# Moving two inverse groups, the W2 split and W4's first loads in a one-core S4 convolution and channel-mixing kernel

## The chip, the cores and the metric

The kernel runs on one core of a Trainium2 chip. Its engines work at the same time, each through its own instructions in order: PE (TensorE, matmuls; PEld are its weight loads), DVE (VectorE), ACT (ScalarE), POOL (GpSimd) and SP (SyncE, which here only issues DMAs). They wait for each other by semaphores. The metric is device time in microseconds (us) of one execution, lower is better; the number that counts is the median of several timed runs.

## The reference

Input `u` is 2048 x 512 (sequence x channels), all in float32. Cut to what matters:

```python
mod = (_silu(c) @ w_mod).reshape(c.shape[0], 6, 1, -1)
sa, ca, ga, sb, cb, gb = (mod[:, 0], mod[:, 1], mod[:, 2], mod[:, 3], mod[:, 4], mod[:, 5])
h = _layernorm(x, axis=-1) * (1 + ca) + sa
x = x + ga * S4(h)            # long convolution along the sequence, by rfft / irfft of length 4096
h = _layernorm(x, axis=-1) * (1 + cb) + sb
x = x + gb * MLP(h)

def MLP(x):
    h = _gelu(_layernorm(x) @ w1)                  # 512 x 512
    hs = shift_quarters(h, (+1, -1, +2, -2)) @ w2  # each quarter of the channels shifted along the sequence
    x1 = x + hs
    return x1 + _gelu(_layernorm(x1) @ w3) @ w4    # 512 x 1376, 1376 x 512
```

## The kernel before

The whole kernel is one function, `body`, whose instructions are written in the order in which each engine takes them (`tc.manual_schedule()`), so the place of a call in the code is its place in every queue. A value read by matmul at full precision is held as two parts, a rounded high one and the rest (`w1h`/`w1l`, `nh`/`nl`, `wh`/`win`); a product then takes three matmuls per tile. Its stages:

1. **Kernel and input spectra, first half** (to about 207 us): the convolution kernel is built by sines and exponentials, `u` is normalized and transformed, partial spectra go to a scratch tensor `VU`. Loads without a reader nearby hang in `side[k]`, calls made behind turn `k` of a loop of 33. Among them POOL copies `w3` and `w4` in eight pieces into scratch tensors (`WD`, traced as `Dw`, L519).
2. **16 spectrum steps** (loop at L1096; `n` 0 to 15, two halves `jh` of the channels, eight `kc` each). In step `n`, PE makes the kernel's spectrum (`spectrum_k`, L667), DVE the complex product (`multiply`: `ma`, `mb` at L678 and L679, `zc` at L683), PE transforms the product of the step before back (`back`, L693, evicted to `z` by ACT and stored to `ZT`), then makes the input's spectrum of the next step (`spectrum_u`, L644, evicted to `us`). `load_inv` brings one group of `ZT` for the last transform, and `inverse(jh, g)` does it: 8 matmuls in the code, each traced as two (L722, tiles `py` and `ld`), then two adds on DVE into `X2`, the running sum `x` (traced as `KX`, L725). There are four groups `g` in each half. Groups 0, 1, 2 of half 0 stand in steps 11, 12, 13, group 3 behind the loop. W1 and W2 are loaded in halves into a `ld` block by SP (L738), and split one step later: ACT rounds to `w1h`/`w2h` (L120, the line of all ACT operations), DVE takes the difference (L744). W1 is split in steps 9 and 10, the first half of W2 in step 15, its second half in the head.
3. **The head** (L1141 to L1250): the second half's groups arrive from `ZT`, and meanwhile the token mixer starts on groups of 256 tokens in the order 7, 0, 1, 2, 3. `keep(n)` (L1139) issues `n` matmuls whose result nobody reads. `half_stat` and `first_stats` take the statistics of `x` (L772, L777 and L758, L759; POOL finishes them to `rs`, L753 and L754). `mix_mod1` and `mix_mod2` modulate on DVE (L762, L765) and take new statistics, POOL makes `rs` and `nm` of them, `mix_norm` normalizes on ACT (`h`), `transposed` turns `h` on PE (L790, into `pT0` and `pT1`), `parts_of` splits it into `nh` (ACT) and `nl` (DVE, L798), `mix_half` multiplies by W1 (L825, L826 and L828; tile `pm`) and stores the result `go` to the scratch tensor `GD`, in SP's queue (L837). For groups 7 and 0 POOL also copies a halo (L846 to L852). `chan_load` reads the shifted quarters back (`win`, L860), `chan_split` splits them, `chan_sum` multiplies by W2 (L879 to L882). `load_w(c)` loads a third of W3 and of W4 from the scratch tensors in place, into the tile that becomes the low part; `split_w` splits later.
4. **Eight channel groups** (`chan`, from about 391 us): the remaining tokens through W1, W2, W3 and W4.

`ldp` is a ring of 7 blocks of 512 KB for `vu`, W1, W2 and the loads of `ZT`; a load waits until the readers of the block seven places back are through. `psy` holds two tiles `py`. An inverse half takes one of them until its add is done.

## Time and profile before

| | |
|---|---|
| median of 3 timed runs | 710.89 us (709.84 to 711.97) |
| the profiled execution | 707.85 us |
| its span, first to last instruction | 706.1 us |
| PE busy | 668.3 us, 95% of the span |
| DVE, ACT, POOL busy | 500.5, 335.6, 91.8 us |
| granted TensorE clock | 1.00 throughout |
| DMA | 85.51 MB, mean 121 GB/s |

Rows of a timeline give the start in us, the time in us, engine, line of the code, operation, output tile `<-` inputs, shapes and count; a bracket gives how long the engine idled ahead of it and what ended that. Rows of the chain give start, time and what it was. A busy engine is only of interest where others wait for it: each step and each stretch of the head has its own.

### The profile page before, as it was taken

Reading aid. Unit: us, or ns where it says so; the run is one execution under the profiler, and the core shown is the slowest. Engines: PE = TensorE matmul, PEld = TensorE weight load, DVE = VectorE, ACT = ScalarE, POOL = GpSimd, SP = SyncE. Lnnn points to the kernel's source line nnn. Section 1 sums busy time; section 2 is a strip of 40 time slices with the busy share of each in tenths; the row PEclk is TensorE's granted clock in tenths of the full one; section 3 lists DMA queues with packets and bytes.
Section 4 is the critical chain, followed back from the end, with each engine's and each line's share of the span. In section 5 each row is a group of like instructions: output and inputs, shape, how many; then the busy total and the mean of one; then the engine's idle time right before and its main releaser. Section 6 shows DMA issues by size and latency. Waiting matters only on the chain.

```text
span 706.1 us, 16836 instructions
## 1 busy us (share of the span) xinstructions
PE 668.3 (95%) x7083; PEld 516.8 (73%) x7083; DVE 500.5 (71%) x827; ACT 335.6 (48%) x553; POOL 91.8 (13%) x203
## 2 busy tenths in 40 slices
PE   1999999999999999997999899999999999999997
PEld 0456655665578665663778789899898988989896
DVE  7899999999986766867888868467454536354522
ACT  3978898888956354541443632314132221213120
POOL 4011121021000010001562101001110000000000
PEclk9999999999999999999999999999999999999999
DMA  8903274636349996955468111011110201011011
GB/s 281 291 3 94 78 213 120 181 102 194 70 122 337 269 284 234 337 193 198 163 204 293 61 31 31 16 51 26 46 44 16 64 13 38 23 31 31 0 31 31
DMA packets 56627, 85.51 MB, mean 121 GB/s; under 512 B 5508, under 2 KB 43400, under 8 KB 54888
## 3 DMA queue, kind: packets, MB, share of 16 engines
q1 hardware_dynamic: 52536, 66.87, 33.1%
q0 software_dynamic: 3136, 16.52, 6.6%
q8 instruction: 56, 0.92, 0.6%
q10 hardware_dynamic: 880, 1.05, 0.5%
q14 instruction: 19, 0.16, 0.1%
HBM read 58.20 MB, written 31.85 MB: 128 GB/s over the span
## 4 chain that ended last, share of the span: by engine, by line
PE 48%; DMA 2%; DVE 2%; ACT 1%; issue 1%; SPq 0%; POOL 0%; ACTq 0%; DVEq 0%
PE pm L825 7%; PE pm L826 7%; PE pm L828 7%; PE pa L949 6%; PE pa L941 6%; PE pa L942 6%; PE ph L879 2%; PE ph L880 2%; PE ph L882 2%; PE pT L790 2%; DMA ld<-ZT 1%; PE pT L1139 1%; PE py L722 1%; DMA GD<-go 0%; DMA win<-GD 0%
## 5 line engine op out<-in xcount | busy, mean ns | idle before, releaser
L120 ACT ACTIVATE gh<-pm 128x512 fp32r<-128x512 f32 (+1 forms) x48 | 26.9, 561 | 200.6 <-PE pm L828 200.6
L825 PE MATMUL pm<-nh,w3h 128*128 128x256 f32 (+1 forms) x352 | 85.8, 279 | 0.9 <-ACT nh L120 0.9
L826 PE MATMUL pm<-nh,w3l 128*128 128x256 f32 (+1 forms) x352 | 85.6, 279 | 0.1
L933 DVE TENSOR_TENSOR gl<-gf,gh 128x512 fp32r<-128x512 f32 (+1 forms) x48 | 30.9, 643 | 68.3 <-ACT gf L120 68.3
L941 PE MATMUL pa<-w4h,gh 128*128 128x512 f32 (+1 forms) x176 | 69.6, 395 | 0.0
L942 PE MATMUL pa<-w4l,gh 128*128 128x512 f32 (+1 forms) x176 | 68.9, 392 | 0.0
L825 PEld LDWEIGHTS pm<-nh,w3h 128*128 128x128 f32 (+1 forms) x352 | 65.3, 185 | 2.6 <-ACT nh L120 1.1
L826 PEld LDWEIGHTS pm<-nh,w3l 128*128 128x128 f32 (+1 forms) x352 | 65.2, 185 | 2.2 <-DVE w3l L744 0.5
L828 PE MATMUL pm<-nl,w3h 128*128 128x256 f32 (+1 forms) x352 | 54.8, 277 | 0.0
L949 PE MATMUL pa<-w4h,gl 128*128 128x512 f32 (+1 forms) x176 | 48.1, 390 | 0.8 <-DVE gl L933 0.8
L753 POOL TENSOR_TENSOR rs<-mv,eps_t 128x1 f32<-128x1 f32 (+1 forms) x39 | 11.9, 305 | 278.3 <-DVE mv L759 266.5
L457 PE MATMUL xx<-MG,ON 64*128 64x512 f32 x160 | 47.0, 389 | 0.0
L458 PE MATMUL xx<-MG,ON 64*128 64x512 f32 x160 | 47.0, 389 | 0.0
L828 PEld LDWEIGHTS pm<-nl,w3h 128*128 128x128 f32 (+1 forms) x352 | 46.6, 185 | 0.2 <-DVE nl L798 0.2
L885 DVE TENSOR_TENSOR h<-h,ph 128x512 f32<-128x512 f32 x16 | 11.0, 687 | 45.1 <-PE ph L882 45.1
L120 ACT ACTIVATE z<-pz 128x512 f32<-128x512 f32 x32 | 17.4, 594 | 50.5 <-issue 23.2
L475 DVE SCALAR_TENSOR_TENSOR e<-tr,p 128x512 f32<-128x512 f32 x64 | 41.1, 683 | 0.4 <-ACT tr L120 0.4
L678 DVE TENSOR_TENSOR ma<-pk,us 128x512 f32<-128x512 f32 x32 | 21.9, 686 | 25.8 <-issue 13.2
L507 PEld LDWEIGHTS kp<-e,e 128*32 128x32 f32 x2048 | 30.1, 110 | 13.1 <-issue 6.8
L949 PEld LDWEIGHTS pa<-w4h,gl 128*128 128x128 f32 (+1 forms) x176 | 33.0, 188 | 8.3 <-DVE gl L933 1.2
L485 DVE TENSOR_TENSOR e<-tr,m 128x1024 f32<-128x1024 f32 x32 | 39.0, 1219 | 0.0
L484 DVE TENSOR_TENSOR e<-tr,p 128x1024 f32<-128x1024 f32 x32 | 39.0, 1219 | 0.0
(230 smaller groups left out, 1754.6 us busy)
## 6 DMA issues: line engine op xcount, KB each, us to landing
VU<-vs SPq DMA_DIRECT2D x64, 128.0 KB, 3.3
ld<-VU SPq DMA_DIRECT2D x16, 512.0 KB, 12.0
ZT<-z POOLq DMA_DIRECT2D x15, 512.0 KB, 6.0
ld<-ZT SPq DMA_DIRECT2D x12, 512.0 KB, 5.5
Dw<-in_w POOLq DMA_DIRECT2D x8, 688.0 KB, 4.7
xu<-in_u SPq DMA_DIRECT2D x16, 256.0 KB, 8.1
KX<-in_u SPq DMA_DIRECT2D x16, 256.0 KB, 12.1
GD<-go SPq DMA_DIRECT2D x16, 256.0 KB, 2.2
```

The source lines that it names most:

```text
L120: return S.activation(out, in_, f, bias=bias, scale=scale)
L457: T.matmul(x[:, :512], la, ma, start=(i == 0), stop=(i == len(ops) - 1))
L458: T.matmul(x[:, 512:], lb, mb, start=(i == 0), stop=(i == len(ops) - 1))
L475: V.scalar_tensor_tensor(e0[:, 1, a], tr[:, 1, 0], 1.0 - 2.0 * a, mg[:, a], op0=OP.mult, op1=OP.mult)
L484: V.tensor_mul(e0[:, 0], tr[:, 0, 0:1].to_broadcast([128, 2, 512]), mg)
L485: V.tensor_mul(e1.rearrange("p r d q -> p r (d q)"), tr[:, :, 1], m1s[0][:, u % 2:u % 2 + 1].to_broadcast([128, 2, 512]))
L825: T.matmul(p, wh[:, k, c], hi[k], start=(k == 0), stop=False)
L826: T.matmul(p, wl[:, k, c], hi[k], start=False, stop=False)
L828: T.matmul(p, wh[:, k, c], lo[k], start=False, stop=(k == 3))
L941: T.matmul(acc[i], gh[:m, e, s], W4h[:m, f], start=(f == 0), stop=False)
L942: T.matmul(acc[i], gh[:m, e, s], W4l[:m, f], start=False, stop=False)
L949: T.matmul(acc[i], gl[:m, e, s], W4h[:m, f], start=False, stop=(f == 10))
```

## The change

- Inverse group 1 of half 0 leaves step 12: its matmuls are issued in step 15 between the last two `back`s, its adds behind the loop's last DVE work. Group 2 leaves step 13 and stands behind the last `back`, ahead of group 3. Their loads are issued in steps 13 and 14.
- W2 is copied by POOL into a scratch tensor in the first stage (two more calls in `side`), loaded from there in step 12, straight into the tile that becomes its low part, and split in steps 14 and 15.
- `half_stat` of blocks 0 to 3 moves from the head into step 12. `keep(14)` becomes `keep(6)`, `keep(22)` becomes `keep(14)`.
- In the head, one `transposed` order changes (both tiles of one half of `h` first), two inverse halves of group 2 of half 1 change places with parts of the mixer, `mix_mod2(2, 0)` and `mix_mod2(3, 0)` go ahead of the transposes and `nl` of the group before.
- `load_w` is divided: the first third of W4 is loaded behind `chan_load(0)` instead of ahead of two `GD` stores.

```diff
-    WD = {k: dpool.tile(list(A[k].shape), F32, name="D" + k) for k in ("w3", "w4")}
+    WD = {k: dpool.tile(list(A[k].shape), F32, name="D" + k) for k in ("w2", "w3", "w4")}
...
+    for k in range(2):
+        side[28 + 3 * k].append(lambda i=k * 256: P.dma_start(WD["w2"][i:i + 256], A["w2"][i:i + 256]))
...
+    def inverse_parts(jh, g):
+        return [inv_half(jh, g, i, psy, "py") for i in range(2)]
+
     def inverse(jh, g):
-        for i in range(2):
-            inv_half(jh, g, i, psy, "py")()
+        for f in inverse_parts(jh, g):
+            f()
...
-        for k in range(4):
+        for j in range(2):
             for i in range(2):
-                T.transpose(ps[k // 2][:, k % 2, i * 128:i * 128 + 128], x[:, i, k * 128:k * 128 + 128], ident)
+                for k in range(2 * j, 2 * j + 2):
+                    T.transpose(ps[j][:, k % 2, i * 128:i * 128 + 128], x[:, i, k * 128:k * 128 + 128], ident)
...
-                W2h, W2l, ldw2 = weights(pw2, A["w2"], 512, 512, "w2", 4)
+                W2h, W2l, ldw2 = weights(pw2, WD["w2"], 512, 512, "w2", 4)
...
             if n > 0:
                 back(*steps[n - 1])
+            if n == 15:
+                i1 = inverse_parts(0, 1)
...
-            if n in (8, 9, 14):
-                split = (ldw1 if n < 10 else ldw2)(two, n % 2 * 2, 2)
-            if 9 <= n < 13:
-                load_inv(0, n - 9)
-            if 11 <= n < 14:
-                inverse(0, n - 11)
+            if n in (8, 9):
+                split = ldw1(two, n % 2 * 2, 2)
+            if n == 9:
+                load_inv(0, 0)
+            if n == 11:
+                inverse(0, 0)
+            if n == 12:
+                w2s = [ldw2(None, 2 * i, 2) for i in range(2)]
+                for b in range(4):
+                    half_stat(b, 0)
+            if n == 13:
+                load_inv(0, 1)
+                load_inv(0, 2)
+            if n == 14:
+                load_inv(0, 3)
+            if n in (14, 15):
+                w2s.pop()()
+        for f in i1:
+            f()
         back(*steps[15])
...
+        inverse(0, 2)
         inverse(0, 3)
-        for b in (14, 15, 0, 1, 2, 3, 4, 5, 6, 7):
+        for b in (14, 15, 4, 5, 6, 7):
             half_stat(b, 0)
         load_inv(1, 1)
-        split = ldw2(two, 2, 2)
-        keep(14)
+        keep(6)
...
-        keep(22)
+        keep(14)
...
-        split()
...
+        a20 = inv_half(1, 2, 0, psy, "py")
         mix_half(0, hl, 0)
-        a20 = inv_half(1, 2, 0, psy, "py")
         mix_norm(1)
         first_stats(2)
         mix_half(0, hl, 1)
+        mix_mod1(2)
+        mix_mod2(2, 0)
+        hl = parts_of(transposed(mh.pop(1)[0]))
         a21 = inv_half(1, 2, 1, psy, "py")
-        mix_mod1(2)
-        hl = parts_of(transposed(mh.pop(1)[0]))
-        mix_mod2(2, 0)
...
-        load_w(0)
+        load_w3(0)
...
         chan_load(0)
+        load_w4(0)
         mix_mod1(3)
+        mix_mod2(3, 0)
         hl = parts_of(transposed(mh.pop(2)[0]))
-        mix_mod2(3, 0)
         mix_mod2(3, 1)
-        load_w(1)
-        load_w(2)
+        load_w3(1)
+        load_w4(1)
+        load_w3(2)
+        load_w4(2)
```

How the change moves instructions is seen on two engines at the end of the steps and on one in the head; a name's number tells buffers apart. First PE from the end of step 15 on, before (`pz` are the two `back`s, `py` and `pm` inverse halves, `pT<-w1h` the `keep`s, `pT<-ident` the transposes of group 7):

```order
L693 MATMUL pz<-zc_4498,Gm 128x512 x2
L693 MATMUL pz<-zc_4499,Gm 128x512 x2
L693 MATMUL pz<-zc_4575,Gm 128x512 x2
L693 MATMUL pz<-zc_4576,Gm 128x512 x2
L722 MATMUL py<-ld,FI 64x256 x8
L1139 MATMUL pT_4671<-w1h 128x512 x14
L722 MATMUL py<-ld,FI 64x256 x8
L722 MATMUL pm<-ld,FI 64x256 x8
L1139 MATMUL pT_4719<-w1h 128x512 x22
L790 MATMUL pT_4783<-ident,h_4742 128x128 x4
```

The same place in the changed kernel:

```order
L695 MATMUL pz<-zc_4479,Gm 128x512 x2
L695 MATMUL pz<-zc_4480,Gm 128x512 x2
L724 MATMUL py<-ld,FI 64x256 x8
L695 MATMUL pz<-zc_4562,Gm 128x512 x2
L695 MATMUL pz<-zc_4563,Gm 128x512 x2
L724 MATMUL py<-ld,FI 64x256 x16
L1161 MATMUL pT_4676<-w1h 128x512 x6
L724 MATMUL py<-ld,FI 64x256 x8
L724 MATMUL pm<-ld,FI 64x256 x8
L1161 MATMUL pT_4716<-w1h 128x512 x14
L796 MATMUL pT_4772<-ident,h_4731 128x128 x4
```

Group 1's eight matmuls now stand between the two `back`s, group 2's eight with group 3's behind them, and 16 of the 36 throwaway matmuls are gone.

DVE over the same steps, before (`ma` and `mb` are the products of step 15, `zc` their sums, `w2l` the split of W2, `KX` the adds of an inverse group):

```order
L683 TENSOR_TENSOR zc_4499<-mb 128x4x64
L678 TENSOR_TENSOR ma<-pk_4541,us 128x512
L679 TENSOR_TENSOR mb<-pk_4541,us 128x512
L678 TENSOR_TENSOR ma<-pk_4542,us 128x512
L679 TENSOR_TENSOR mb<-pk_4542,us 128x512
L683 TENSOR_TENSOR zc_4575<-ma 128x4x64
L683 TENSOR_TENSOR zc_4576<-mb 128x4x64
L683 TENSOR_TENSOR zc_4575<-ma 128x4x64
L683 TENSOR_TENSOR zc_4576<-mb 128x4x64
L744 TENSOR_TENSOR w2l<-ld,w2h 128x512 x2
L725 TENSOR_TENSOR KX<-py,KX 128x2x256 x2
```

And in the changed kernel:

```order
L685 TENSOR_TENSOR zc_4480<-mb 128x4x64
L749 TENSOR_TENSOR w2l<-w2l,w2h 128x512 x2
L680 TENSOR_TENSOR ma<-pk_4528,us 128x512
L681 TENSOR_TENSOR mb<-pk_4528,us 128x512
L680 TENSOR_TENSOR ma<-pk_4529,us 128x512
L681 TENSOR_TENSOR mb<-pk_4529,us 128x512
L685 TENSOR_TENSOR zc_4562<-ma 128x4x64
L685 TENSOR_TENSOR zc_4563<-mb 128x4x64
L685 TENSOR_TENSOR zc_4562<-ma 128x4x64
L685 TENSOR_TENSOR zc_4563<-mb 128x4x64
L749 TENSOR_TENSOR w2l<-w2l,w2h 128x512 x2
L727 TENSOR_TENSOR KX<-py,KX 128x2x256 x6
```

A split of W2 now stands ahead of the last products as well as behind them, and six adds follow where there were two.

DVE in the head around `nl` of group 1, before (first rows: statistics of `x` for group 2 and `mix_mod1(2)`; `h<-h,rs` with the two rows behind it is `mix_mod2`):

```order
L777 BN_AGGR mv_77<-st_79 128x2
L762 SCALAR_TENSOR_TENSOR h_5033<-KX,mv_77,modg 128x512 x2
L798 TENSOR_TENSOR nl_5051<-pT_5039,nh_5049 128x512
L798 TENSOR_TENSOR nl_5052<-pT_5040,nh_5050 128x512
L765 SCALAR_TENSOR_TENSOR h_5033<-h_5033,rs_78,modg 128x512
L758 BN_STATS st<-h_5033 128x6
L759 BN_AGGR mv<-st 128x2
L725 TENSOR_TENSOR KX<-py,KX 128x2x256
```

And in the changed kernel:

```order
L782 BN_AGGR mv_78<-st_80 128x2
L767 SCALAR_TENSOR_TENSOR h_5013<-KX,mv_78,modg 128x512 x2
L770 SCALAR_TENSOR_TENSOR h_5013<-h_5013,rs_79,modg 128x512
L763 BN_STATS st<-h_5013 128x6
L764 BN_AGGR mv<-st 128x2
L804 TENSOR_TENSOR nl_5039<-pT_5027,nh_5037 128x512
L804 TENSOR_TENSOR nl_5040<-pT_5028,nh_5038 128x512
L727 TENSOR_TENSOR KX<-py,KX 128x2x256
```

`mix_mod2(2, 0)`, three instructions, moved ahead of the two `nl`, and with it DVE's wait for POOL's `rs`. Around `nl` of group 2 the same holds for `mix_mod2(3, 0)`.

More of the change, by code (lines that the diff above doesn't have):

```diff
@@ L1069, in body, with load_w3, load_w4 @@
     splits = []
-    def load_w(c):
-        for c0, fs in ((0, range(4)), (512, range(4, 8)), (1024, range(8, 11)))[c:c + 1]:
-            for i in range(4):
-                splits.append(ldw3(None, i, 1, c0, min(c0 + 512, 1376)))
-            for f in fs:
-                splits.append(ldw4(None, f))
+    def load_w3(c):
+        for i in range(4):
+            splits.append(ldw3(None, i, 1, 512 * c, min(512 * c + 512, 1376)))
+    def load_w4(c):
+        for f in range(4 * c, min(4 * c + 4, 11)):
+            splits.append(ldw4(None, f))
     def split_w(n):
```

## The prediction

> **What bounds the kernel now.** I read the page's busy shares first, then the stretches of the steps the change touches, then the chain that ended last, and then each engine's timeline there.
>
> ```profile
> PE 668.3 (95%) x7083; PEld 516.8 (73%) x7083; DVE 500.5 (71%) x827; ACT 335.6 (48%) x553; POOL 91.8 (13%) x203
> 299.02:306.45 7.43, 7.43 (x106) 4.63 (x106) 5.21 (x12) 2.80 (x8) 0.53 (x1) 1.00 0.94 285
> 313.88:319.58 5.70, 5.63 (x88) 3.33 (x86) 3.82 (x9) 2.80 (x8) 0.53 (x1) 1.00 0.24 95
> ```
>
> The first row is the page's; in the others the columns are the stretch and its length, then busy time of PE, PE's loads, DVE, ACT and POOL, clock, DMA share, GB/s. They run from one eviction of `z` to the next, so each is one spectrum step, number 12 and number 14. PE is busy 7.43 of 7.43 us where a step carries an inverse group and 5.63 of 5.70 where it carries none; DVE and ACT have room. The steps are PE's. The stretch behind them is not:
>
> ```profile
> 317.52 1.99 PE L693 MATMUL pz<-zc,Gm 64*128 64x512 f32 x8
> 321.33 1.99 PE L693 MATMUL pz<-zc,Gm 64*128 64x512 f32 x8 [1.82 <-ACT w2h L120]
> 325.12 3.47 PE L1139 MATMUL pT<-w1h 128*128 128x512 f32 x14
> 330.19 2.14 PE L722 MATMUL py<-ld,FI 128*64 128x256 f32 x10 [1.60 <-DMA ld<-ZT]
> ...
> 324.48 2.25 DMA ZT<-z
> 329.34 6.58 DMA ld<-ZT
> 335.97 1.08 PE pm L722 x6
> 337.05 5.23 PE pT L1139 x22
> 342.41 1.06 PE pT L790 x8
> 339.59 0.82 ACT L120 ACTIVATE h<-h,nm,rs 128x512 f32<-128x512 f32 x1 [0.38 <-POOL nm L815]
> ```
>
> The upper rows are PE's timeline, then rows of the chain, then one of ACT. PE waits 1.82 us for the last product, fills 3.47 us with 14 throwaway matmuls, waits 1.60 us for the loads of `ZT`, and later runs 22 more throwaways. Their end at about 342.3 releases the transposes of group 7 at 342.41, though their input `h` was complete at 339.59 + 0.82 = 340.41. From there on PE is the path, with short waits.
>
> **The change part by part.** Times are on the clock of the profile; behind the last `back` they are counted as if that had started at 321.33 as before, so that each part's own gain shows.
>
> *Inverse groups 1 and 2 leave steps 12 and 13.* Each of these steps falls to the length of the step without a group: 2 x (7.43 - 5.70) = 3.46 us **earlier**. Four `half_stat` enter step 12 on DVE:
>
> ```profile
> 325.99 3.37 DVE L772 BATCH_NORM_STATS2 st<-KX 128x6 f32<-128x256 f32 x10
> 317.70 0.69 DVE L678 TENSOR_TENSOR ma<-pk,us 128x512 f32<-128x512 f32 x1 [1.88 <-issue]
> ```
>
> 4 x 0.337 = 1.35 us, which fits in the 1.88 us that DVE idles before a product in a step without a group, so nothing; without that cover it would be the 1.35 us.
>
> *The first W2 split moves into step 14*, in DVE's order ahead of the last step's products. The W1 split stands so already, two products earlier:
>
> ```profile
> 278.30 0.69 DVE L678 TENSOR_TENSOR ma<-pk,us 128x512 f32<-128x512 f32 x1 [1.88 <-issue]
> 283.53 1.29 DVE L744 TENSOR_TENSOR w1l<-ld,w1h 128x512 fp32r<-128x512 f32 x2 [1.40 <-ACT w1h L120]
> 284.74 0.68 DVE L678 TENSOR_TENSOR ma<-pk,us 128x512 f32<-128x512 f32 x1
> ```
>
> DVE waits for ACT's halves behind the `us` evictions, and the next product starts 6.44 us after the one before instead of 5.70: 0.74 us late. In the middle of the steps that cost nothing, since PE took the product two operations later. In the last step `back` waits for exactly this product (the 1.82 us above), and everything behind it: 0.74 us **later**, bounds 0 (ACT done earlier) and 1.29 (the whole split). The second split stays where it was, behind the last product.
>
> *Group 1 between the last two `back`s.* Its 1.73 us of PE starts at 317.52 + 1.99 = 319.5 and ends at 321.2; `back` is released at 321.33 + 0.74. It is hidden. *Group 2 behind `back`*: 1.73 us in place of 8 throwaways (8 x 0.24 = 1.92). DVE gets four more adds of 0.7 us there; with its six statistics it is done at about 329.9, while the next add is this one:
>
> ```profile
> 331.80 0.69 DVE L725 TENSOR_TENSOR KX<-py,KX 128x512 f32<-128x512 f32 x1 [2.44 <-PE py L722]
> ```
>
> So 1.9 us of room, nothing. The ring of `ld` blocks now lets one half of the first loads wait for group 2's matmuls, about 325.2, before the 324.48 + 2.25 = 326.7 at which these loads can be issued anyway. The W2 load that stood in SP's queue behind the loads of group 1 makes room for a load of group 2 of the same 512 KB: nothing.
>
> *22 throwaways become 14.* They start at 337.05, where the loads set it, and end at 337.05 + 14 x 0.24 = 340.4, when `h` is complete (340.41). The transposes start there and not at 342.41: 2.0 us **earlier**; bounds 0 (`h` that much later) and 2.0.
>
> *The rest of the head.* DVE's order and its waits before:
>
> ```profile
> 341.08 1.41 DVE L762 SCALAR_TENSOR_TENSOR h<-KX,mv,modg 128x512 f32<-128x512 f32 x2
> 343.70 1.29 DVE L798 TENSOR_TENSOR nl<-pT,nh 128x512 fp32r<-128x512 f32 x2 [1.22 <-ACT nh L120]
> 348.09 1.28 DVE L744 TENSOR_TENSOR w2l<-ld,w2h 128x512 fp32r<-128x512 f32 x2
> 362.23 1.29 DVE L798 TENSOR_TENSOR nl<-pT,nh 128x512 fp32r<-128x512 f32 x2 [1.99 <-ACT nh L120]
> ...
> 352.62 0.39 PE L825 MATMUL pm<-nh,w1h 128*128 128x256 f32 x1 [0.25 <-ACT nh L120]
> 369.53 0.98 PE L790 MATMUL pT<-ident,h 128*128 128x128 f32 x7 [1.08 <-ACT h L120]
> 377.35 0.50 PE L879 MATMUL ph<-w2h,wh 128*128 128x512 f32 x1 [0.44 <-ACT wh L120]
> ```
>
> Group 7's `nl` can come only when DVE is through at 342.5, so DVE gains 1.2 us there where PE gains 2.0, and 1.28 more where the W2 split is gone: PE waits some 0.75 us for group 0's second `h`. Half group 4 of the inverse now fills the 0.25 us wait for group 0's `nh` (the first of three such waits). For group 1, DVE does `mix_mod2(2, 0)`, 0.74 + 0.70 + 0.18 = 1.6 us, ahead of `nl`, where it used to idle 1.99. Its `rs` would come at about 359.65 (the next rival), so `nl` starts at 361.3 and its halves end at 361.95 and 362.55; PE, through with the high products at 360.9, loses about 1.4 us to them, and for group 2 by the same count about 0.7. In exchange the waits of 1.08 and 0.44 go, the three of 0.25, and part waits of 0.3 and 0.4 inside the groups: 2.9 us of waits gone, 2.9 new. I take 0, bounds 2.0 earlier (few of the new waits) and 1.6 later (all of them grown as in rival 1).
>
> *W4's first loads behind `chan_load(0)`* take 1.0 MB out of the way of the `GD` transfers, which ends the 0.44 us wait counted above. *Two more copies to a scratch tensor and W2 from there*:
>
> ```profile
> Dw<-in_w POOLq DMA_DIRECT2D x8, 688.0 KB, 4.7
> ld<-in_w SPq DMA_DIRECT2D x4, 512.0 KB, 10.1
> ```
>
> Each copy is a POOL issue in the first stage, smaller than the eight there, and POOL is 13% busy. The loads stand behind `vu` of step 15 and need 10.1 us by the second row, two steps' time; they are used in step 14. Nothing for either; up to 0.3 us for the copies.
>
> Sum: -3.46 + 0.74 - 2.0 + 0 = **-4.7 us**. The profiled execution took 707.85 us, so it would take 703.1. The median of the three timed runs, 710.89, is 3.0 above that execution; from it I forecast **706.2 us**. A difference of about 0.3% (2.1 us) is what a measurement of this kernel can tell from no change.
>
> **The rivals.** *1. DVE waits for POOL ahead of `nl`.* `mix_mod2` needs POOL's `rs`, which stands behind the copies of the halo in POOL's order:
>
> ```profile
> 359.66 0.62 POOL L753 TENSOR_TENSOR rs<-mv,eps_t 128x1 f32<-128x1 f32 x1
> 360.36 0.55 POOL L754 TENSOR_TENSOR rs<-rs,pw 128x1 f32<-128x1 f32 x1
> 365.21 0.19 POOL L753 TENSOR_TENSOR rs<-mv,eps_t 128x1 f32<-128x1 f32 x1 [2.78 <-DVE mv L759]
> ```
>
> The same operation takes 0.19 or 0.62 us. If POOL does not come earlier with the rest, `nl` starts only at 360.36 + 0.55 + 1.6 = 362.5, 1.2 us later, group 2 loses 0.8 likewise, and the 2.0 us of the throwaways are gone: total -2.7, 708.2 us. For it: the copies stand there as before. Against: `go`, which the copies wait for, also comes 1.3 us earlier. [...]
>
> *2. The weights arrive in one burst.* 19 loads, 4.6 MB, now stand ahead of the `GD` stores of group 2, before it was 15, 3.5 MB:
>
> ```profile
> 373.64 1.85 SPq L738 DMA_DIRECT2D w3l<-Dw  x4
> 382.62 8.20 SPq L837 DMA_DIRECT2D GD<-go  x4
> 388.10 0.60 ACT L120 ACTIVATE go<-pm 128x512 f32<-128x512 f32 x1 [5.11 <-DMA GD<-go]
> 389.84 0.60 ACT L120 ACTIVATE go<-pm 128x512 f32<-128x512 f32 x1 [0.62 <-PE pm L828]
> ...
> 372.00:374.00 2.00, 2.00 (x19) 1.94 (x18) 1.93 (x5) 0.00 (x0) 0.28 (x1) 1.00 0.60 184
> 374.00:386.00 12.00, 11.56 (x75) 10.27 (x74) 9.69 (x17) 5.68 (x9) 3.38 (x10) 1.00 1.02 333
> ```
>
> Before, ACT waited 5.11 us for such a store, hidden with 1.7 us to spare (the next `go` came at 389.84). With `chan_load(0)` some 2 us earlier the burst starts near 371 and, at the 333 GB/s of the second window, ends near 385, the stores 1 us later: hidden, since that `go` is then due at 387.7. If the burst starts no earlier than before, it ends 3 us later than it did, ACT is some 3.4 us late, and the total is -1.4, 709.5 us. *The same mechanism ends on the other side* where the burst is slow: at a rate r the stores land 4.6 MB / r + 1 us after 371. The gain is eaten up when that is 387.7 + 4.7 = 392.4, at r = 225 GB/s, and it is slower by over 0.3% below 204 GB/s; at the first window's 184 it lands at 397, 9.3 us late, total +4.6: **715.5 us**. For it: that window's rate and its DMA share of 0.60. Against: SP stood between two bursts there, and behind it the share is 1.02.
>
> *3. It doesn't do what it says*: the moved groups only change place, because the wait for `ZT`'s loads moves with them and the steps stay at 7.43. Then only term 3 less 0.74 is left, -1.3, 709.6 us. The step of 5.70 us and PE's empty 1.82 speak against it.
>
> *4. Better*: no cost from the W2 split and fewer new waits, -6 us, 704.9.
>
> **How the numbers follow.** Forecast 0.50, rival 1 0.20, rival 2 0.10, its slower end 0.07, rival 3 0.07, better 0.06. Faster by over 0.3%: forecast, better and rival 1, 0.76; within 0.3%: rivals 2 and 3, 0.17; slower 0.07. The range takes in the better case, rivals 1 to 3 and not the slow end: 704.2 to 709.6. The forecast's own is 705.2 to 707.4.
>
> **What would show it.** Steps 12 and 13 of 5.7 us; the last product 6.4 us behind the one before; group 1's matmuls in front of the last `back` with PE idle for 0.8 us and not 1.82; the second run of throwaways ending within 0.2 us of `h`; waits of about 1 us on `nl` for groups 1 and 2; PE's wait on `wh` gone. From the first `pm<-nh,w3h` on, the two traces should run in parallel, 4.7 us apart. It is wrong if that distance differs at the end, if the last step loses over 1.3 us, or if ACT's `go` of group 3 waits past PE.

## The result and the profile after

| | before | after |
|---|---|---|
| median of the timed runs, made together | 709.68 us (706.52 to 713.69, 10 runs) | 705.40 us (702.23 to 706.82, 10 runs) |
| the profiled execution | 707.85 us | 706.57 us |
| its span | 706.1 us | 704.8 us |
| granted TensorE clock, mean | 1.000 | 0.996 |

The ratio of the times is 0.9945, with a 95% interval of 0.9928 to 0.9962: 4.3 us or 0.55% faster. The forecast was 706.2 us, in a range of 704.2 to 709.6.

The two profiled executions differ by 1.3 us only, and that has to be understood before anything else is read from them. ACT's timeline of before, with the eviction of `z` of steps 1, 2, 10 and 15, the last, and then the first product with W3 in PE's:

```profile
239.16 1.09 ACT L120 ACTIVATE z<-pz 128x512 f32<-128x512 f32 x2 [2.86 <-PE pz L693]
246.13 1.09 ACT L120 ACTIVATE z<-pz 128x512 f32<-128x512 f32 x2 [4.13 <-DMA ZT<-z]
291.60 1.09 ACT L120 ACTIVATE z<-pz 128x512 f32<-128x512 f32 x2 [1.88 <-PE pz L693]
323.37 1.08 ACT L120 ACTIVATE z<-pz 128x512 f32<-128x512 f32 x2 [1.66 <-issue]
...
391.49 0.38 PE L825 MATMUL pm<-nh,w3h 128*128 128x256 f32 x1 [0.87 <-ACT nh L120]
```

The same places after:

```profile
239.18 1.09 ACT L120 ACTIVATE z<-pz 128x512 f32<-128x512 f32 x2 [2.86 <-PE pz L695]
247.60 1.08 ACT L120 ACTIVATE z<-pz 128x512 f32<-128x512 f32 x2 [5.58 <-DMA ZT<-z]
293.76 1.09 ACT L120 ACTIVATE z<-pz 128x512 f32<-128x512 f32 x2 [1.88 <-issue]
322.81 1.08 ACT L120 ACTIVATE z<-pz 128x512 f32<-128x512 f32 x2 [2.39 <-issue]
...
389.97 0.39 PE L831 MATMUL pm<-nh,w3h 128*128 128x256 f32 x1 [2.94 <-ACT nh L120]
```

Up to 239 us the two run together within 0.02 us: the two copies of W2 on POOL cost nothing. Then ACT waits for stores to `ZT` in steps 2 to 7, whose code the change leaves as it was, and by step 10 this execution of after has lost 293.76 - 291.60 = 2.16 us by chance. In the 14 profiled executions of this study the `z` of step 10 comes anywhere between 290.3 and 295.9 us. Behind the first product with W3, on the other hand, all 14 need 314.6 to 314.8 us to the end of the span. What the change does lies between these two places, and there the traces can be compared to about 0.1 us: 391.49 - 291.60 = 99.89 us before, 389.97 - 293.76 = 96.21 us after, 3.68 us less. With 2.16 lost ahead and 0.2 behind, this is the 1.3 us of the two spans.

Stretches of the steps after, in the columns of the prediction's first rows; they are steps 12 and 13:

```profile
301.19:306.89 5.70, 5.70 (x90) 3.48 (x90) 5.13 (x13) 2.80 (x8) 0.53 (x1) 1.00 1.08 363
306.89:312.60 5.71, 5.71 (x90) 3.49 (x90) 3.83 (x10) 2.80 (x9) 0.53 (x1) 1.00 0.86 269
```

Steps 12 and 13 fell from 7.43 us to the 5.70 of a step without a group, with the four statistics of DVE in the first of them (5.13 us busy). PE's timeline behind them:

```profile
318.15 1.95 PE L724 MATMUL py<-ld,FI 128*64 128x256 f32 x16
320.77 1.99 PE L695 MATMUL pz<-zc,Gm 64*128 64x512 f32 x8 [0.67 <-DVE zc L685]
322.82 3.85 PE L724 MATMUL py<-ld,FI 128*64 128x256 f32 x32
...
330.20 1.08 PE L724 MATMUL py<-ld,FI 128*64 128x256 f32 x8 [1.94 <-DMA ld<-ZT]
...
339.98 0.87 PE L796 MATMUL pT<-ident,h 128*128 128x128 f32 x6 [0.30 <-ACT h L120]
360.62 1.09 PE L834 MATMUL pm<-nl,w1h 128*128 128x256 f32 x4 [0.83 <-DVE nl L804]
367.21 0.39 PE L831 MATMUL pm<-nh,w1h 128*128 128x256 f32 x1 [0.35 <-ACT nh L120]
```

Group 1 (x16 at 318.15) fills the time in which the last `back` waits, which falls from 1.82 to 0.67 us. Group 2 follows the last `back` (half of the x32 at 322.82) in place of throwaways. Group 7's transposes wait 0.30 us for `h` behind 14 throwaways, so these are no longer the limit. In the mixer PE idles 0.83 us for `nl` and 0.35 for `nh`, and the waits of 1.08 us for `h` and 0.44 us for `wh` are gone. The one bad place is the 2.94 us at 389.97. SP's timeline, the chain, and ACT's timeline there:

```profile
380.08 2.00 SPq L743 DMA_DIRECT2D w4l<-Dw  x3
382.50 6.80 SPq L843 DMA_DIRECT2D GD<-go  x4
...
382.50 4.70 DMA GD<-go
...
387.31 0.60 ACT L120 ACTIVATE go<-pm 128x512 f32<-128x512 f32 x1 [7.99 <-DMA GD<-go]
388.32 0.59 ACT L120 ACTIVATE go<-pm 128x512 f32<-128x512 f32 x1
389.32 1.09 ACT L120 ACTIVATE nh<-pT 128x512 fp32r<-128x512 f32 x2
```

The stores of group 2's `go` are issued at 382.50, behind the burst of 19 weight loads, and land 4.70 us later; only then may ACT write group 3's `go` into their buffer, and `nh`, for which PE waits, stands two `go` further back in ACT's order. A late `go` of this kind is what rival 2 of the prediction priced.

### The profile page after: what moved, and what is told of

It reads as the page before. It is cut to its first block, busy times and chain, and to the rows that moved or that the text cites. A ratio compares the mean times of both kernels' runs of the same rounds, so it can differ in the third digit from the quotient of the medians.

```text
span 704.8 us, 16806 instructions
## 1 busy us (share of the span) xinstructions
PE 666.8 (95%) x7067; PEld 516.0 (73%) x7067; DVE 500.4 (71%) x827; ACT 335.3 (48%) x553; POOL 92.2 (13%) x205
## 4 chain that ended last, share of the span: by engine, by line
PE 79%; DVE 11%; DMA 3%; ACT 3%; issue 2%; POOL 1%; SPq 0%; DVEq 0%; ACTq 0%; POOLq 0%
PE pm L834 7%; PE pm L831 7%; PE pm L832 7%; PE xx L457 7%; PE pa L947 6%; PE pa L948 6%; PE pa L955 6%; PE pk L669 4%; PE pk L646 4%; PE pz L695 4%; PE kp L507 4%; PE pu L434 2%; PE ph L886 2%; PE ph L888 2%; PE ph L885 2%; DMA w4l<-Dw 2%
## 5 line engine op out<-in xcount | busy, mean ns | idle before, releaser
L120 ACT ACTIVATE p<-xx 128x1024 f32<-128x1024 f32 (+1 forms) x40 | 37.5, 980 | 2.1 <-PE xx L258 0.4
```

The source lines that it names most:

```text
L120: return S.activation(out, in_, f, bias=bias, scale=scale)
```

## The experiments

Each was timed beside the kernel before, so its ratio is to that (whose medians in these batches were 708.69 to 709.00 us, and 709.68 beside "after"). The medians carry the spread of steps 2 to 7, some 1.5 us either way, so the stretches of the trace decide. In the table, in us: from `z` of step 10 to the last `z`, from there to the first `go` of group 2 on ACT, from there to PE's first product with W3, and the sum of the three. "Again" is the changed kernel once more.

| kernel | steps | to `go` | to W3 | sum | median | ratio (95%) |
|---|---|---|---|---|---|---|
| before | 31.77 | 50.75 | 17.37 | 99.89 | 709.68 | |
| after | 29.05 | 48.37 | 18.79 | 96.21 | 705.40 | 0.9945 (0.9928 to 0.9962) |
| again | 29.05 | 48.52 | 18.73 | 96.30 | 705.15 | 0.9943 (0.9925 to 0.9961) |
| 1. W4 first | 29.05 | 48.31 | 18.06 | 95.42 | 705.33 | 0.9957 (0.9932 to 0.9981) |
| 2. stores first | 29.05 | 49.08 | 16.66 | 94.79 | 703.95 | 0.9935 (0.9912 to 0.9958) |
| 3. split in step 13 | 28.33 | 48.41 | 18.07 | 94.81 | 704.52 | 0.9949 (0.9927 to 0.9972) |
| 4. 22 throwaways | 29.04 | 49.84 | 18.57 | 97.45 | 706.78 | 0.996 (0.994 to 0.998) |
| 5. before with 14 | 31.77 | 49.51 | 17.48 | 98.76 | 707.79 | 0.9983 (0.9964 to 1.0001) |
| 6. groups back | 32.50 | 48.53 | 17.97 | 99.00 | 710.00 | 1.001 (0.999 to 1.0029) |
| 6. once more | 33.78 | 49.00 | 18.17 | 100.95 | 709.57 | 1.0014 (0.9996 to 1.0032) |
| 7. `nl` first | 29.04 | 47.99 | 19.37 | 96.40 | 705.11 | 0.9942 (0.9923 to 0.9961) |
| 8. filled wait | 29.05 | 48.28 | 18.93 | 96.26 | 706.10 | 0.9964 (0.9937 to 0.999) |
| 2 and 3 | 28.33 | 48.31 | 16.68 | 93.32 | 703.20 | 0.9923 (0.9898 to 0.9947) |
| 2, 3 and 7 | 28.33 | 48.01 | 16.72 | 93.06 | 702.84 | 0.9897 (0.9873 to 0.9922) |

One thing disturbs the second column. With only 6 throwaways ahead, PE waits some 1.9 us for the loads of `ZT` (1.94 us in the timeline above), and in six of the ten executions with these 6 (again, 1, 2, 4, 7, and 2, 3 and 7) the granted clock was 0.50 right behind that wait; with 14 there it was so in none of four. Ten and four are too few to say that the 6 are the cause. But it shows in the end of group 7's transposes: 17.9 to 18.1 us behind the last `z` where the clock stayed at 1.00 (after, 3, 8, and 2 with 3), and 18.0, 18.2, 18.7, 19.0 and 19.0 in runs 1, again, 2, 2 with 3 and 7, and 7 (run 4 has other throwaways). From that end on the traces repeat to 0.1 us: it is 30.3 us to the `go` in after, again, 1, 2, 3, 8, and 2 with 3.

**The changed kernel again.** 

> The changed kernel once more, for a second profile of it: the waits of 0.67 us ahead of the last back and of about 2.9 us ahead of the first pm<-nh,w3h come back within 0.5 us if they belong to the kernel and not to that one execution, and the steps 3 to 8, the same code in both kernels, differ by up to 2 us from one execution to the next if their waits on loads are what spreads the times.

The time came out alike, and so did every wait: 0.67, 0.82, 0.35 and 2.88 us. A wait that comes back to 0.1 us belongs to the program, and the 2.9 us do.

**1. The first loads of W4 back behind those of W3.**

```diff
         load_w3(0)
+        load_w4(0)
...
         chan_load(0)
-        load_w4(0)
```

> The changed kernel with the first third of W4 loaded ahead of the two GD stores again, all else as changed. If the burst of 19 weight loads holds back the stores of group 2, 15 loads stand ahead of them now: they are issued 1 to 3 us earlier against the kernel's own mixer, PE's wait of 2.94 us ahead of the first pm<-nh,w3h falls to 0 to 2 us, and the clock behind it stays at 1.00 or dips less; on the other side chan_load(0) lands later and PE's wait on wh, which the change removed, comes back with 0 to 1 us. Net 1 to 3 us faster than the changed kernel, some 702 to 704 us. If that wait has another cause (ACT's own order of go, w3h and nh), it stays at 2.9 us and the kernel is the same or slower than the changed one.

PE waits 1.17 us for `wh` again and only 0.87 us in front of the first product with W3. So this part of the change trades one wait for the other: it takes away 1.17 us and brings 2.94 - 0.87 = 2.07 us, some 0.8 us lost in the stretch. That is less than the 1 to 3 us expected, and the median does not resolve so little.

**2. The last third of W3 and W4 behind the stores of group 2's `go`.**

```diff
-        load_w3(2)
-        load_w4(2)
...
         mix_half(2, hl, 1)
+        load_w3(2)
+        load_w4(2)
```

> The changed kernel with the last thirds of W3 and W4 (7 loads, 1.4 MB) moved in SP's queue behind the two GD stores of group 2. Burst theory: the stores are issued behind 12 weight loads, at about 377 instead of 382.5 us, land before 384, ACT's go of group 3 no longer waits for them past PE (the 7.99 us wait falls to 4 or less), PE's 2.94 us wait falls under 1 us and the clock does not dip: 2 to 4 us faster than the changed kernel, 701 to 703.5 us. Rival (ACT's order sets the wait, or the stores are slow of themselves): PE still waits over 2 us there and the time does not move.

SP's and ACT's timelines of this run:

```profile
376.22 1.08 SPq L843 DMA_DIRECT2D GD<-go  x2
377.57 3.86 SPq L743 DMA_DIRECT2D w3l<-Dw  x4
...
383.19 0.60 ACT L120 ACTIVATE go<-pm 128x512 f32<-128x512 f32 x1 [4.10 <-DMA GD<-go]
385.94 0.60 ACT L120 ACTIVATE go<-pm 128x512 f32<-128x512 f32 x1 [1.63 <-PE pm L834]
```

Counted from the last `z`, the first stores are issued at 54.4 us (376.22 - 321.85) and no longer at 59.7, the first `go` of group 3 comes 2.75 us ahead of the second, and the second waits for PE's product again and no longer for a store. The stores still release ACT only 7 us after their issue (376.22 and 383.19); what helps is that they are issued 5 us sooner. PE's wait is back at 0.87 us and the last of the three stretches falls from 18.8 to 16.7 us. Only the order in SP's queue differs, so the price of the burst is shown: 2.1 us. The sum of the stretches falls by 1.4 only, since in this execution the clock dipped ahead of group 7's transposes, which end 18.73 us behind the last `z` and not 18.04.

**3. W2's first split in step 13 instead of step 14.**

```diff
-            if n in (14, 15):
+            if n in (13, 15):
                 w2s.pop()()
```

> The changed kernel with the first W2 split one step earlier, in step 13 instead of 14. If its place ahead of the last products costs what the trace says, the last products start 5.70 us behind the ones before instead of 6.44, PE's wait ahead of the last back falls from 0.67 to about 0, and up to that back 0.7 us are gained (the ones ahead of it are not slowed: PE has 5.7 us steps either way). At the end of the kernel the gain may be eaten by the wait for the GD stores, whose time is set by the weight loads: 0 to 0.7 us faster than the changed kernel. Rival: the delay is made up or comes from the load of W2, then nothing moves at the last back.

DVE's and PE's timelines of this run:

```profile
308.58 1.29 DVE L749 TENSOR_TENSOR w2l<-w2l,w2h 128x512 fp32r<-128x512 f32 x2 [1.40 <-ACT w2h L120]
...
318.40 1.99 PE L695 MATMUL pz<-zc,Gm 64*128 64x512 f32 x8
```

DVE waits as long as before for ACT, but one step earlier, where PE has other work, and the last `back` has no wait in front of it. The steps take 28.33 instead of 29.05 us, 0.72 less. The 0.7 us in the third stretch go with stores that are issued 0.5 us sooner behind the last `z` in this execution (59.16 instead of 59.69 us); with the same queue that time varied between 18.0 and 18.9 us.

**4 and 5. 22 throwaways in the changed kernel, and 14 in the kernel before.** The edit is the number in `keep`, at the second of its two places.

> The changed kernel with keep(22) in front of the transposes of group 7, as in the kernel before. If the keep-warm matmuls were on the path (the term of -2.0 us): eight more 128x512 matmuls, 22 in 5.5 us instead of 14 in 3.5 us; the wait of 0.3 us for h goes, the transposes of group 7 start 1.7 us later, the start of go of group 2 comes 50.0 to 50.3 us after the last z instead of 48.4 to 48.5 us, and the time is 707.0 us beside 705.3 us for the changed kernel. Rival: the stores of group 2's gates behind the burst of weight loads set the end of the head; the delay is then taken from the wait of 2.9 us for nh, the first product with W3 comes where it came (67.2 us after the last z) and the time stays at 705.3 us. Between them lies the case that the burst itself starts later, since it waits for the W1 buffers that the same matmuls free; then the wait of 2.9 us stays and the whole 1.7 us are lost.

> The kernel before with keep(14) instead of keep(22), and nothing else of the change. If the keep-warm matmuls were on the path there by themselves: go of group 2 comes 1.3 to 2.0 us earlier behind the last z than the 50.75 us of the kernel before, and the time is 707.2 us beside 709.0 us. Rival: without the inverse groups behind step 15, the wait on the last group's ld (2.77 us in the kernel before) or the wait for h grows by what the keep gives up, go stays within 0.5 us, and the time is 709 us.

In the changed kernel eight throwaways more cost 1.3 to 1.5 us to the `go` and 1.2 us to the product with W3; in the kernel before eight fewer gain 1.24 and 1.13 us. Both lie below the 2.0 of the prediction, which was worked out for an earlier place, the transposes. PE's timeline of the kernel before with 14:

```profile
341.28 0.98 PE L790 MATMUL pT<-ident,h 128*128 128x128 f32 x7 [0.31 <-ACT h L120]
350.90 0.98 PE L790 MATMUL pT<-ident,h 128*128 128x128 f32 x7 [0.74 <-ACT h L120]
```

Counted from the last `z` (324.08 here), group 7's transposes end 18.18 us later, before 20.10: 1.92 us are gained there. But group 0's `h` does not come earlier, and PE waits 0.74 us for it, where it used to wait for nothing. Freed time is partly given back at the next wait.

**6. Groups 1 and 2 back in steps 12 and 13**, with their loads in steps 10 to 12 and `keep(14)` ahead of the last group, twice.

```diff
-            if n == 15:
-                i1 = inverse_parts(0, 1)
...
-            if n == 9:
-                load_inv(0, 0)
-            if n == 11:
-                inverse(0, 0)
+            if 9 <= n < 13:
+                load_inv(0, n - 9)
+            if n in (11, 12, 13):
+                inverse(0, n - 11)
...
-        inverse(0, 2)
         inverse(0, 3)
```

> The changed kernel with groups 1 and 2 of the inverse back in steps 12 and 13 and their loads in steps 10 to 12, keep(14) ahead of the transposes of the last group. If the first term holds: z of steps 12 and 13 is 7.43 us after the one before it again instead of 5.70 us, 3.46 us in all, the matmuls of groups 1 and 2 are no longer ahead of the last group behind step 15, and the time is 708.3 to 708.8 us, beside 705.3 us for the changed kernel. Rival (the matmuls of the two groups cost the same wherever they stand, or the wait for ld behind step 15 was as long with them): the time stays within 1 us of 705.3 us, and the wait on ld at 328 us grows by what the steps lose.

> The kernel with the two inverse groups back in steps 12 and 13 once more. Its stretch from step 10 to the first product with W3 was 2.75 us longer than that of the changed kernel, its median 4.7 us longer. If the other 2 us are the spread of steps 3 to 8 (where the code is the same in all), this median comes out nearer to 705.3 + 2.75 = 708.0 us, and z of step 10 in the profile before 294.5 us. Rival: the earlier loads of the two groups cost time in steps 3 to 10 each time; then the median is 709.5 to 710.5 us again and z of step 10 comes at 294 us or later.

The steps take 3.45 us more in the first execution, which is the prediction's first term (3.46) to the hundredth. In the second they take 4.73 us more. Its PE timeline, and a window of 2 us there (stretch, length, busy PE, PEld, DVE, ACT, POOL, granted clock, DMA share, GB/s):

```profile
322.30 3.30 PE L695 MATMUL pz<-zc,Gm 64*128 64x512 f32 x8 [2.55 <-DVE zc L685]
...
324.00:326.00 2.00, 2.00 (x6) 0.33 (x5) 0.00 (x0) 0.38 (x1) 0.00 (x0) 0.50 0.00 0
```

Without group 1 between the two last `back`s, PE waits 2.55 us there, about the 0.67 plus the 1.95 us that the group took. In this execution the clock fell to 0.50 behind that wait, and the eight matmuls took 3.30 us instead of 1.99. The medians lie 4.2 to 4.9 us above that of the changed kernel, more than the 3.5 of the steps; the half clock, in some executions, is a part of the rest that is seen, and how much more of it is spread stays open. `z` of step 10 came at 294.6 and at 291.8 us, so the loads do not delay it each time.

**7. The second half of `mix_mod` behind `nl`, as before.**

```diff
         mix_mod1(2)
-        mix_mod2(2, 0)
         hl = parts_of(transposed(mh.pop(1)[0]))
+        mix_mod2(2, 0)
...
-        mix_mod2(3, 0)
         hl = parts_of(transposed(mh.pop(2)[0]))
+        mix_mod2(3, 0)
```

> The changed kernel with the second half of mix_mod of groups 2 and 3 behind the transposes and nl of the group before it, as in the kernel before. Theory (rival 1 of the prediction): DVE's wait of 0.71 us for POOL's rs in front of h delays nl, and PE waits 0.83 us for nl instead of 0.25 us for nh in group 1: with the order of before the wait of 0.83 us falls to 0.25 to 0.39 us, go of group 2 comes up to 0.6 us earlier, and the time is 704.7 to 705.3 us. Rival: h of group 2 then comes later than its transposes need it, PE waits there (0.98 us behind 1.08 us in the kernel before), and the time is 705.3 to 706.5 us.

PE's timeline of this run, and a window behind its wait of 1.98 us on `ld`, ahead of group 7's transposes:

```profile
338.41 0.88 PE L796 MATMUL pT<-ident,h 128*128 128x128 f32 x6 [0.76 <-ACT h L120]
363.85 0.88 PE L796 MATMUL pT<-ident,h 128*128 128x128 f32 x6 [0.67 <-ACT h L120]
...
387.67 0.39 PE L831 MATMUL pm<-nh,w3h 128*128 128x256 f32 x1 [3.52 <-ACT nh L120]
...
328.00:330.00 2.00, 2.00 (x12) 1.16 (x12) 0.24 (x1) 0.00 (x0) 0.00 (x0) 0.50 1.05 342
```

The wait for `nl` is gone, and the wait for `h` has returned, at 0.67 us. The `go` of group 2 comes 0.4 to 0.5 us earlier behind the last `z`, and that hides most of what the order does. The clock dipped in this execution, and group 7's transposes end 18.98 us behind the last `z` (338.41 + 0.88 - 320.31) and not 18.04. From there to the `go` it takes 29.01 us instead of 30.33: with the order of before this piece is 1.3 us shorter, so moving `mix_mod2` ahead of `nl` costs 1.3 us. The wait in front of W3 grows from 2.9 to 3.5 us, and the sum of the three stretches does not fall: what is gained ahead of the stores is for the most part taken by them.

**8. Twelve throwaway matmuls in the wait in front of W3.**

```diff
         r = transposed(n)
+        d = psm.tile([128, 512], F32, name="ph")
+        for _ in range(12):
+            T.matmul(d, W1h[:, 0, :128], W1h[:, 0], start=True, stop=True)
```

> The changed kernel with twelve matmuls (128x512, results unused) that TensorE runs while it waits for nh in front of the first product with W3. They take some 2.6 us and leave the wait as it is, but keep TensorE busy through it. If the half clock behind that wait costs time: the granted clock stays 1.00 from 386 to 402 us, the wait of 0.7 to 0.8 us on DVE's gl does not change, and the time falls by about 1 us to 704.3 us. Rival (the slow matmuls lie in front of a wait on gl that takes up what they lose): from the first product with W3 to the end of the span 314.6 us instead of 314.7 to 314.8 us, and the time stays at 705.3 us. If the twelve end later than nh comes, up to 0.5 us are lost.

The question was what the half clock costs. A window of the changed kernel's first profile, behind its wait of 2.94 us:

```profile
392.00:394.00 2.00, 2.00 (x11) 2.00 (x11) 2.00 (x4) 0.48 (x1) 0.00 (x0) 0.50 0.34 102
```

A window and PE's timeline of the filled kernel:

```profile
390.00:392.00 2.00, 2.00 (x20) 2.00 (x19) 1.97 (x4) 2.00 (x5) 0.00 (x0) 1.00 0.03 8
...
383.19 3.01 PE L1271 MATMUL ph<-w1h 128*128 128x512 f32 x12
386.59 0.38 PE L831 MATMUL pm<-nh,w3h 128*128 128x256 f32 x1 [0.38 <-ACT nh L120]
395.28 1.19 PE L955 MATMUL pa<-w4h,gl 128*128 128x512 f32 x4 [0.82 <-DVE gl L939]
```

With the fill the clock stays at 1.00, and PE waits 0.82 us on `gl` nine microseconds later. In the changed kernel that wait is not there: the slow matmuls took up its 0.8 us. From the first product with W3 to the end it is 314.6 us with the fill and 314.8 without. The half clock costs 0.2 us at most there, and the late stores are the cost of that place. The median, 706.1 us, says nothing against it: its twelve runs lie between 702.5 and 711.0, and the profiled one has a span of 701.2 us, since its `z` of step 10 came at 290.3.

**2 and 3 together, then with 7.**

> The two edits that gained together: the last third of the W3 and W4 loads behind the stores of group 2's gates (alone 703.95 us), and the first split of W2 in step 13 instead of step 14 (alone 704.52 us), beside 705.3 us for the changed kernel. If they lie at separate places, the gains add: 1.3 + 0.7 = 2.0 us, 703.3 us; no wait in front of the last back product, 0.9 us instead of 2.9 us in front of the first product with W3, granted clock 1.00 from 384 to 402 us. Rival: the 0.7 us that the steps gain are lost again in the wait for the last group's ld, which is set by transfers, so that the time stays at 703.9 us.

> The weights behind the stores and W2's first split in step 13 (together 703.2 us), and the second half of mix_mod of groups 2 and 3 behind nl as in the kernel before. Alone, that last edit brought go of group 2 forward by some 0.4 us and the time stayed at 705.1 us, with a wait of 3.52 us for nh. Theory: the stores of group 2's gates took that gain away; without them in the way it reaches the end: go of group 2 0.4 us earlier behind the last z than in the version without it, 0.9 us in front of the first product with W3, 702.8 us. Rival: the last steps of the head are paced by ACT and POOL (the wait is taken up by the next go), so that the first product with W3 comes where it came and the time stays at 703.2 us.

PE's timeline of the last one:

```profile
386.36 0.39 PE L831 MATMUL pm<-nh,w3h 128*128 128x256 f32 x1 [0.87 <-ACT nh L120]
```

Edits 2 and 3 add: 2.9 us in the stretch, 2.0 in the median. With the stores out of the way, edit 7 brings 0.26 us to the sum, where alone it brought nothing. It would bring more: this execution again had a clock of 0.50 behind its wait on `ld`, and group 7's transposes end 18.96 us behind the last `z` instead of 17.99. From there to the product with W3 it takes 45.77 us instead of 47.00, so 1.2 of the 1.3 us now arrive. The medians, 702.84 and 703.20, do not resolve this. The last kernel is the fastest of all, 702.84 us, ratio 0.9897 (0.9873 to 0.9922): about 2.5 us less than the changed kernel.

## Why the prediction was right, and where not

The forecast of 706.2 us stands beside 705.40, and part of that closeness is luck. It started from 710.89, a median of three runs, where ten runs gave 709.68: a start 1.2 us too high. The gain was forecast at 4.7 us where the medians, with their spread, say 4.3 and 3.8 and the traces, from step 10 to the product with W3, 3.6 to 3.7. The two errors partly cancel. The sum is about 1 us too large, and is itself made of errors of both signs:

| term | predicted | measured | by |
|---|---|---|---|
| groups out of steps 12, 13 | -3.46 | -3.45 | windows; run 6, first execution |
| W2's split ahead of the last product | +0.74 | +0.72 | run 3 |
| 22 throwaways to 14, at the end of group 7's transposes | -2.0 | -2.06 | trace; -1.92 by run 5, -1.55 to -1.72 by run 4 |
| from there to the first `go` of group 2 | 0, with the next row | -0.32 | trace, 30.65 and 30.33 |
| from that `go` to W3 | | +1.42 | trace; of it +2.1 for the stores by run 2, so -0.7 without them |

**The steps** came out as worked out, to 0.02 us: 31.77 - 29.05 = 2.72 us, predicted 3.46 - 0.74. That a step is as long as PE's work in it was read from two rows of the windows, and that the split is hidden everywhere but ahead of the last product from three rows of DVE. Group 1 hid between the last two `back`s as said, with 0.67 us of idle time left for the 0.8 forecast.

**The throwaways** were on the path, and the term was right for the place for which it was worked out: 2.0 us at the transposes. Further on less is left, 1.2 to 1.5 us at the `go` (runs 4 and 5), since in run 5 PE gives 0.74 us back at group 0's `h`. The prediction counted that wait, "some 0.75 us", with the rest of the head.

**The new waits** for `nl` were counted at 1.4 and 0.7 us. PE multiplies by W1 in turns of eight products with `nh` and four with `nl`. PE's timeline after, the start of the first turn and of the second in group 0, then in group 1, and of the second in group 2 (whose first, at 367.21, stands above):

```profile
350.47 0.39 PE L831 MATMUL pm<-nh,w1h 128*128 128x256 f32 x1
352.00 0.28 PE L831 MATMUL pm<-nh,w1h 128*128 128x256 f32 x1
...
358.58 0.39 PE L831 MATMUL pm<-nh,w1h 128*128 128x256 f32 x1
361.55 0.28 PE L831 MATMUL pm<-nh,w1h 128*128 128x256 f32 x1
...
369.51 0.28 PE L831 MATMUL pm<-nh,w1h 128*128 128x256 f32 x1
```

The first turn, 1.53 us in group 0, takes 2.97 us in group 1 and 2.30 in group 2, so 1.44 and 0.77 us are lost, as forecast. The bracket of 0.83 us shows only a part: it stands ahead of the first of the four products with `nl`, and their row itself takes 1.09 instead of 0.64 us, since the second `nl` comes later still. The waits that went were worth 0.3 us more than these and the others that came. Run 7 gives the price of the reordering alone, 1.3 us, and so the rest of the changes up to the `go` must have gained some 1.6; which of them, no run separates.

POOL's `rs` is ready early enough that rival 1 did not happen, though DVE does wait for it. POOL's and DVE's timelines after:

```profile
357.71 0.55 POOL L759 TENSOR_TENSOR rs<-rs,pw 128x1 f32<-128x1 f32 x1
358.49 0.96 POOL L759 TENSOR_TENSOR rs<-rs,pw 128x1 f32<-128x1 f32 x1
...
358.29 0.75 DVE L770 SCALAR_TENSOR_TENSOR h<-h,rs,modg 128x512 f32<-128x512 f32 x1 [0.71 <-POOL rs L759]
```

DVE starts when `rs` is there, at 358.26, 35.45 us behind the last `z`, where the prediction had 36.3. The second `rs` runs beside DVE's modulation and takes 0.96 instead of 0.55 us. The longer of the two times of one operation in rival 1's rows, 0.62 and not 0.19 us, also ran beside a modulation of DVE (358.76 to 360.23 us in the kernel before). POOL lost 0.41 us here, where DVE's instruction had 0.55 us left when POOL's began, and 0.43 us there; what slows POOL in these two places, the traces do not show.

**The step that failed** is "ends near 385, the stores 1 us later: hidden, since that `go` is then due at 387.7". Both of its times were wrong by nearly 2 us. The burst from its first load to the landing of the stores, after and before, and before's stores (issues, size of each, median us to landing, from 380 to 390 us):

```profile
369.23:387.20 17.97, 17.80 (x126) 16.45 (x126) 11.78 (x20) 5.68 (x9) 3.72 (x9) 1.00 0.92 306
373.64:388.02 14.38, 13.94 (x95) 12.65 (x94) 11.32 (x21) 5.68 (x9) 4.61 (x12) 1.00 0.93 307
...
GD<-go SPq DMA_DIRECT2D x3, 256.0 KB, 5.4
```

*The landing.* It took 17.97 us, at 306 GB/s, and not 13.8 us at 333 plus 1. The trace of before had this: its 15 loads and the same stores took 14.38 us at 307 GB/s, the stores alone 5.4 us (4.70 after); the 333 was the rate of the busy middle, and like the others it counts all transfers. As an estimate, four loads of 256 KB more are 3.4 us at 307 GB/s, which makes 17.8. In the clock of the prediction, 0.56 us ahead of this trace's, the burst starts at 369.8, even earlier than the 371 forecast, and the stores land at 387.8, not 386.

*The due time.* What must not be late is the first `go`; the one due with PE's product is the second, which stands 1.0 us behind it (387.31 and 388.32). So the spare of before was 0.7 us and not 1.7. In run 2 the second `go` starts 0.78 us before PE's idle time begins (385.94, and 387.59 - 0.87 = 386.72). By this the second `go` was due after the change at 389.97 - 2.94 - 0.78 = 386.25 and the first at 385.24, which is 385.8 in the prediction's clock. The stores came 2.07 us later. That this equals the growth of PE's wait, 0.87 to 2.94, lies in the reckoning; the independent measure is run 2, with 2.13 us.

The prediction's own last sign of being wrong, "if ACT's `go` of group 3 waits past PE", is thus there. Rival 2 stood at 0.10 and put ACT 3.4 us late if the burst started no earlier than before. It started 3.85 us earlier behind the last `z` (46.42 us, before 50.27), and ACT was late all the same, by 2.1: the effect came, on another condition. That the forecast of the time held is because the rest of the head gained 1.0 us that was not forecast (0.3 and 0.7), which pays half of the stores, and because of the start that was 1.2 us too high. Run 7 shows besides that a gain right ahead of the stores brings little while they are late.

## What to carry to other kernels

A store that frees a buffer belongs ahead of a burst of loads in its queue (2.1 us here, by run 2); where it stands behind one, take its landing time from such a place (4.7 and 5.4 us here, 2.2 in the median) and its due time from the first instruction that needs the buffer, not from the one on the critical path behind it. A gain is worth what the next wait leaves of it: 1.9 us of removed matmuls came to 1.2, and the 1.3 us of an earlier `nl` to nothing in the sum until the stores were out of the way. The bracket of a merged row gives only the idle time ahead of its first instruction; what a late input costs is read from the distance of two instructions around it (1.44 us, and the bracket said 0.83). Where a stage spreads by several microseconds between executions, compare stretches between two fixed instructions and not spans, which said 1.3 us here where the stretch said 3.7; and look at the clock in each stretch first, since one dip hid nearly 1 us of run 7's gain.

## What the runs showed of the hardware that was not expected

**Transfers behind a burst.** The DMA groups of after (issues, size of each, median us to landing), over the whole run and then from 380 to 390 us alone:

```profile
GD<-go SPq DMA_DIRECT2D x16, 256.0 KB, 2.2
...
GD<-go SPq DMA_DIRECT2D x4, 256.0 KB, 4.7
```

The same store takes 2.2 us in the median of all sixteen and 4.7 us behind the loads (5.4 in the kernel before), although the DMA engines moved 328 GB/s before it (369.20 to 382.50 us) and 241 while it was on its way. Of the last three loads ahead of it in SP's queue, those of W4 issued from 380.08 us on, the two of 256 KB took 5.0 us in the median, about as long. What holds these stores back, no trace shows; run 2 shows what their place in the queue is worth, 2.1 us.

**The half clock** came behind waits of 3.52, 2.94, 2.80, 2.41, 2.30 and 2.20 us in front of W3, but not behind one of 2.88 us in the repeated kernel, nor behind 2.55 us in the last step of run 6, first execution. In the wait for the loads of `ZT` behind the last `z` it came behind 1.85, 1.90, 1.93, 1.98, 2.03 and 2.37 us, but not behind 1.83, 1.87, 1.90, 1.94, 2.00 and 2.35. So the length of the wait alone does not decide it. Once there, it lasted as long each time: in the windows of 2 us around the one of 392 to 394 the clock was 0.84, 0.50 and 0.81, together 0.85 of a window lost, and at half clock that takes 1.7 windows, by this estimate 3.4 us; the same 0.85 comes out in the repeated kernel from 96 to 102 us (0.80, 0.50, 0.85), in 2, 3 and 7 from 328 to 334 us (0.98, 0.50, 0.67) and in run 6, second execution, from 322 to 328 us (0.71, 0.50, 0.94). It also came with hardly any wait. PE's timeline of the repeated kernel, and a window there:

```profile
97.07 0.70 PE L457 MATMUL xx<-C,T0S 64*128 64x512 f32 x1 [0.34 <-ACT p L120]
...
98.00:100.00 2.00, 2.00 (x12) 1.63 (x10) 2.00 (x3) 1.99 (x4) 0.00 (x0) 0.50 1.26 488
```

PE idled 0.34 us, and the clock was 0.50 for these 2 us. The first profile of the changed kernel has the same wait of 0.34 us there, at 97.08, and no dip. The same dip stands at this place in runs 2, 3 and 6 (second execution); in these four the `z` of the first step then came at 234.2 to 234.3 us, and at 233.0 to 233.5 us in the nine executions without a dip in the first stage (the one left, 2 and 3, had its dip at 55 us). The code is the same there. What brings the half clock stays open here: the same wait of 0.34 us was followed by it in one execution and not in the other.
